# DeltaNet then MLP mixer: folded first recurrence with its state in PSUM, keys before queries, more work on GpSimd, and a new order

## The chip, the cores and the metric

The kernel runs on one core of one Trainium2 chip. A core has five engines that work side by side, each through its own queue in order: PE (TensorE, matrix products), DVE (VectorE), ACT (ScalarE), POOL (GpSimd) and SP (SyncE, which issues the transfers here). Products are written to PSUM, and DVE and ACT carry them to SBUF, the on-chip memory. The metric is the device time of one execution in microseconds, as the median of several runs.

## What is computed

The first half is a DeltaNet recurrence for 4 batches, 8 heads, 768 tokens and a head size of 48. The second is an MLP mixer over tokens (768 to 256 and back) and channels (384 to 1536 and back).

```python
def _attn_ref(q, k, v, beta) -> np.ndarray:
    ...
    k_n = k / (np.linalg.norm(k, axis=-1, keepdims=True) + 1e-06)
    state = np.zeros((B, H, D, D), dtype=np.float32)
    ...
    for t in range(S):
        kt, vt, bt = (k_n[:, :, t], v[:, :, t], beta[:, :, t, None])
        y[:, :, t] = np.einsum('bhd,bhde->bhe', q[:, :, t], state)
        v_old = np.einsum('bhde,bhd->bhe', state, kt)
        state = state + bt[:, :, :, None] * np.einsum('bhd,bhe->bhde', kt, vt - v_old)
    return y.astype(np.float32)
...
def _moe_ref(x, w_tok1, w_tok2, w_ch1, w_ch2) -> np.ndarray:
    xt = x.transpose(0, 2, 1)
    h = np.maximum(xt @ w_tok1, 0.0) @ w_tok2
    u = x + h.transpose(0, 2, 1)
    h2 = np.maximum(u @ w_ch1, 0.0) @ w_ch2
    return (u + h2).astype(np.float32)
```

## The kernel before

Tokens are taken in chunks of 64 (C), two chunks to a unit of 128 tokens: six units and twelve chunks for each batch, 24 units and 48 steps in all. Within a chunk the recurrence is solved in matrix form. The products of all keys with all keys (the gram) are masked to a triangle M; the inverse T of the unit triangular matrix gives the chunk's corrected values w = T (V - K S), where S is the state at the chunk's start; S is then changed by K'w and the outputs are read from Q, S and w.

The work is cut into generators, called jobs, each of which issues a few instructions and then yields. One long string, `order`, written into the kernel (L912 on), says which job is advanced next. Since scheduling is manual, each engine's queue holds its instructions in exactly that order; buffers and semaphores decide when each can start. The jobs, with their lines in the kernel before:

- k{u}, `load_kq` (L296): transfers of keys and queries of unit u to `kpad` and `qpad`, and of keys, stacked by chunk, to `kst`; for the first units ACT makes `kst` from `kpad` (L312).
- p{u}, `prep` (L345): squares on ACT (L354), sums on DVE (L357), roots on ACT, then on DVE the addition of a small number (L364), the reciprocal (L368), its square (L369) and the column `cs` = beta times that square (L370); PE turns the keys (L380) and the queries (L395); the mask `mb` is a triangle times `cs` (L388) and the scaled keys are `kst` times `cs` (L399), on DVE for units 0 to 3 (`EARLY_SC`) and on POOL for the others; the gram `p_g` (L408) covers keys and queries together, and DVE evicts it with the mask (L414); `to_parts` (L474) copies 32x32 blocks to where they are inverted.
- i{n}, `invert`: round 0 holds units 0 to 3, round 1 units 4 and 5; both turn blocks in SBUF on DVE (L518, L540, L543) and take back substitution steps of two DVE instructions (L526, L531). From round 2 on, rounds pass through DRAM (L520, L546). h{u} (`join_16`), f{u} (`from_parts`, L493) and j{u} (`join`, PE L592 and L601, ACT L595 and L604) build T of 64x64 from the inverted blocks.
- v{u}, `load_v` (L324): values, scaled on POOL (L329).
- r{t}: `recur_early` (L608) for the twelve steps of the first batch, `recur` (L684) for the other 36. A step of `recur_early` is: `p_k` = K S on PE (L629), V minus that on DVE (L633), `p_w` = T times it on PE (L648), a copy on ACT (L650), `p_s` = K'w on PE (L656), two subtractions from the state on DVE (L660), and the reading `p_y` (L639, L667) with its copies on ACT (L675).
- m{b}, `mixer` (L755): the token products `p_1` (L762), `p_h` (L775) and the transposes `p_ut`, then the channel products `p_c` (L824, relu on ACT L831) and `p_o` (L844, added to the output on DVE L793), in a scheme that makes seven half-size products do for eight, with sums on DVE (L817).
- w{j}, `round_weights` (L206): a piece of the weights comes as 64-bit words (L215) and becomes float32: ACT L220, DVE L221 and L226, ACT L232, POOL L233, and last a flush of tiny values to zero by one DVE instruction (L235). There are 34 pieces (j from 0).
- x and z, `keep_warm` (L162), and y, `warm_tiles` (L171): matrix products on zeros that only keep PE occupied, written to `p_warm` and `p_warm_2`.

PSUM tiles come from rings of banks: two for "prep", two for "seq" (`p_k`, `p_w`, `p_s`), three for "mlp" (one of which `p_warm_2` holds for good).

Every float32 product appears in the trace as two matmul records; a transpose appears as one.

Of the kernel before, what the change touches and what calls it, by code (L numbers as in the profile page):

```python
# [8 lines left out]
FP32 = mybir.dt.float32  # L9
# [4 lines left out]
C = 64  # L14
# [9 lines left out]
def kernel(  # L24
# [83 lines left out]
    EARLY_SC = (0, 1, 2, 3)  # L108
# [9 lines left out]
    mask_f = const.tile([128, 128], FP32, name="mask_f")  # L118
# [41 lines left out]
    p_warm_2 = ps_mlp([128, 4, 128], "p_warm_2")  # L160
# [10 lines left out]
    def warm_tiles():  # L171

        while True:
            for i, r in enumerate(PAR):
                for k, out_r in enumerate(PAR):
                    nc.tensor.matmul(  # L176
                        (p_warm_2 if i == k else p_warm)[out_r, 0], warm[r, 0:C],
                        warm[r, 0:128],
                    )
            yield  # L180
# [25 lines left out]
    def round_weights(dst, src, name):  # L206
# [13 lines left out]
        nc.scalar.activation(lo, lo, ACTF.Copy, scale=2.0**-29)  # L220
        nc.vector.tensor_scalar(  # L221
# [10 lines left out]
        nc.scalar.square(a, a)  # L232
        nc.gpsimd.tensor_tensor(out=f, in0=f, in1=lo, op=ALU.add)  # L233
        yield
        nc.vector.scalar_tensor_tensor(  # L235
            out=dst, in0=a, scalar=(1.125 * 2.0**-15) ** 2, in1=f.bitcast(FP32),
            op0=ALU.is_ge, op1=ALU.mult,
        )
# [3 lines left out]
    def round_pair(j, src):  # L242
# [4 lines left out]
            b[:, 2 * k : 2 * k + 2].rearrange("p j n -> p (j n)"), src, (id(wc2), j)  # L247
# [12 lines left out]
    def pieces_of(dst, src):  # L260
        rows = src.rearrange("(j p) n -> j p n", p=128)
        for n in range(0, dst.shape[2], WP):
            for j in range(dst.shape[1]):
                cut = slice(n, min(n + WP, dst.shape[2]))
                yield round_weights(dst[:, j, cut], rows[j, :, cut], (id(dst), j, n))
# [9 lines left out]
    turning = set()  # L275
# [8 lines left out]
    beta_in = []  # L284
    steps = []
    written = set()
    walked = set()
# [7 lines left out]

    def load_kq(u):  # L296
        assert u < NK or u - NK in masked
        b, c = divmod(u, NCH)
        ksts[u] = kst = loads.tile([128, NP, 2, D], FP32, name="kst", bufs=NK)
        for pad, src in ((kpad, k), (qpad, q)):  # L300
            nc.sync.dma_start(
# [22 lines left out]
    def load_v(u):  # L324
        assert u < 2 or u - 2 in walked
# [19 lines left out]
    def prep(u):  # L345

        assert u < NV or u - NV in walked
        b, c = divmod(u, NCH)
        kp, qp, kst = kpad[u % NK], qpad[u % NK], ksts.pop(u)
# [3 lines left out]
        ksq = work.tile([128, NB, D], FP32, name="ksq", bufs=1)  # L353
# [11 lines left out]
        cs = work.tile([128, NP, 2], FP32, name="cs")  # L365
        rec = work.tile([128, NB], FP32, name="rec")
# [650 lines left out]
```

## Time and profile before

| what | value |
|---|---|
| time, median of three runs | 729.87 us (729.57 to 732.58) |
| span of the profiled execution | 730.9 us |
| PE busy | 700.8 us (96%), 7774 matmul records |
| DVE busy | 439.8 us (60%), 1163 instructions |
| ACT busy | 242.1 us (33%), 569 instructions |
| POOL busy | 99.4 us (14%), 118 instructions |

The profile is one execution. "Busy" adds up the time in which an engine had an instruction under way; PE can be busy with products on zeros. The row PEclk gives the clock that PE was granted, in tenths of full speed. A group of instructions is named by line, engine and operation, with output and inputs by the program's names.

### The profile page before, as it was taken

To read this page: it belongs to the slowest core of one execution; us is meant where nothing else is said; L and a number is where in the kernel's file an instruction comes from. 1 tells how busy PE (TensorE), PEld (TensorE's weight loads), DVE (VectorE), ACT (ScalarE), POOL (GpSimd) and SP (SyncE) were. 2 spreads that over 40 slices of the span, in tenths; PEclk is the share of its full clock that TensorE was granted. 3 is DMA by queue.
4 is the path that set the end of the run, shared out by engine and by line. 5 is a ranking of instruction groups with operands and counts; after the bars stand their busy time and mean duration, and the time that the engine had idled before them with its cause. 6 is when DMAs were issued, how large, how long until landed. Compare 5 with 4: busy or idle time off the path is not lost.

```text
span 730.9 us, 18603 instructions
## 1 busy us (share of the span) xinstructions
PE 700.8 (96%) x7774; PEld 605.5 (83%) x7774; DVE 439.8 (60%) x1163; ACT 242.1 (33%) x569; POOL 99.4 (14%) x118
## 2 busy tenths in 40 slices
PE   8797998999999999999999999999999999999998
PEld 6556886757799988986899898968998986989997
DVE  5998678799796792545965559723776432311212
ACT  6636447443561213432325422123222331020110
POOL 1223035332323010121001201001000000000000
PEclk9987579899899999999999999999999999999999
DMA  9435435564425405255023222131002100000000
GB/s 169 107 85 117 88 72 133 161 140 105 90 66 99 91 1 111 41 109 102 1 60 77 43 59 42 39 70 28 12 28 42 34 12 1 22 0 23 1 22 22
DMA packets 146755, 46.13 MB, mean 63 GB/s; under 512 B 138064, under 2 KB 141136, under 8 KB 146672
## 3 DMA queue, kind: packets, MB, share of 16 engines
q1 hardware_dynamic: 146672, 44.95, 28.7%
q8 instruction: 61, 1.00, 0.6%
q14 instruction: 22, 0.18, 0.1%
HBM read 35.49 MB, written 9.44 MB: 61 GB/s over the span
## 4 chain that ended last, share of the span: by engine, by line
PE 67%; DVE 22%; ACT 3%; issue 3%; DMA 2%; SPq 1%; POOL 0%; ACTq 0%; DVEq 0%; POOLq 0%
PE p_o L844 20%; PE p_c L824 16%; DVE sub L526 6%; DVE x L531 5%; PE p L762 4%; PE p_q L702 4%; PE p_s L728 3%; PE p_w L718 3%; PE p_g L408 3%; PE p_h L775 3%; PE p_z L592 2%; PE p_x L601 2%; PE p_warm L166 1%; PE p_warm L176 1%; DVE gm L414 1%
## 5 line engine op out<-in xcount | busy, mean ns | idle before, releaser
L824 PE MATMUL p_c<-u_t,wc 128*128 128x256 f32 x864 | 195.6, 381 | 0.0
L824 PEld LDWEIGHTS p_c<-u_t,wc 128*128 128x128 f32 x864 | 161.2, 191 | 20.9 <-issue 0.3
L844 PE MATMUL p_o<-wc,r 128*128 128x192 f32 x720 | 128.5, 328 | 1.1 <-ACT u_t L789 0.6
L844 PEld LDWEIGHTS p_o<-wc,r 128*128 128x128 f32 x720 | 116.6, 190 | 3.1 <-ACT u_t L789 1.1
L831 ACT ACTIVATE r<-p_c 128x512 f32<-128x512 f32 x72 | 42.7, 596 | 156.1 <-PE p_c L824 156.1
L793 DVE TENSOR_TENSOR xb<-xb,p_o 128x192 f32<-128x192 f32 x84 | 29.3, 350 | 69.8 <-PE p_o L844 69.5
L526 DVE TENSOR_TENSOR sub<-x 128x84 f32<-128x84 f32 (+24 forms) x178 | 59.0, 332 | 14.6 <-DMA x<-n_dram 10.0
L531 DVE TENSOR_TENSOR x<-x,sub 128x84 f32<-128x84 f32 (+24 forms) x178 | 59.9, 336 | 6.1
L721 ACT COPY rw_bd<-p_w 64x192 f32<-64x192 f32 x72 | 22.4, 311 | 99.1 <-PE p_w L718 98.1
L844 PE MATMUL p_o<-wc,s 128*128 128x192 f32 x288 | 51.0, 329 | 2.5 <-DVE xb L793 2.5
L233 POOL TENSOR_TENSOR w_f<-w_f,d 128x384 uint32<-128x384 uint32 (+1 forms) x34 | 35.0, 1030 | 124.5 <-DVE w_f L226 65.3
L329 POOL TENSOR_TENSOR v_st<-v_st,nrm 128x384 f32<-128x384 f32 x24 | 20.1, 840 | 226.1 <-DMA v_st<-in_v_dram 122.0
L844 PEld LDWEIGHTS p_o<-wc,s 128*128 128x128 f32 x288 | 46.8, 190 | 3.7 <-DVE xb L793 3.3
L817 DVE TENSOR_TENSOR s<-r 128x384 f32<-128x384 f32 x24 | 13.9, 578 | 53.6 <-ACT r L831 53.6
L388 POOL TENSOR_TENSOR mb<-mask_c,cs 128x512 f32<-128x512 f32 x20 | 22.6, 1129 | 136.6 <-DVE cs L370 121.9
L414 DVE TENSOR_TENSOR gm<-p_g,mb 128x512 f32<-128x512 f32 x48 | 31.4, 684 | 15.6 <-PE p_g L408 11.5
L408 PE MATMUL p_g<-kqt 64*64 64x128 f32 x768 | 30.8, 304 | 7.3 <-ACT kqt L397 7.3
L702 PEld LDWEIGHTS p_q<-s_bd,kqt 128*128 128x128 f32 x264 | 33.9, 195 | 4.5 <-issue 2.4
L702 PE MATMUL p_q<-s_bd,kqt 128*128 128x96 f32 x264 | 36.0, 281 | 1.3 <-DVE s_bd L741 0.7
L736 DVE TENSOR_TENSOR s_bd<-s_bd,p_s 48x192 f32<-48x192 f32 x60 | 21.4, 357 | 25.9 <-PE p_s L728 25.0
L706 DVE TENSOR_TENSOR rw_bd<-p_q,v_st 64x192 f32<-64x192 f32 x66 | 23.0, 349 | 20.2 <-PE p_q L702 14.1
L728 PEld LDWEIGHTS p_s<-rw_bd,gm 128*112 128x112 f32 x288 | 32.9, 178 | 2.7 <-issue 0.3
(111 smaller groups left out, 999.3 us busy)
## 6 DMA issues: line engine op xcount, KB each, us to landing
d<-in_moe_w_ch_dram SPq DMA_DIRECT2D x24, 384.0 KB, 3.4
kpad<-in_k_dram SPq DMA_DIRECT2D x24, 192.0 KB, 3.7
qpad<-in_q_dram SPq DMA_DIRECT2D x24, 192.0 KB, 4.1
v_st<-in_v_dram SPq DMA_DIRECT2D x96, 48.0 KB, 2.6
out_dram<-xb SPq DMA_DIRECT2D x24, 192.0 KB, 2.0
kst<-in_k_dram SPq DMA_DIRECT2D x80, 48.0 KB, 2.9
n_dram<-gm SPq DMA_DIRECT2D x72, 32.0 KB, 1.9
gm<-w_dram SPq DMA_DIRECT2D x72, 32.0 KB, 2.2
```

What stands on the lines that cost most here:

```text
L233: nc.gpsimd.tensor_tensor(out=f, in0=f, in1=lo, op=ALU.add)
L408: nc.tensor.matmul(p_g[cc][PAR[i ^ cc], p], kqt[PAR[i], 2 * p + cc, 0], kqt[PAR[i], 2 * p + cc],)
L414: nc.vector.tensor_tensor(out=blocks(gm)[:, :, cc, 0 : 2 * C].rearrange("s p (two n) -> s p two n", two=2), in0=p_g[cc], in1=mb[:, :, cc, ...
L526: nc.vector.tensor_tensor(out=tmp, in0=y[:, :, 0:s, s : s + 1].to_broadcast([n, k, s, w]), in1=y[:, :, s : s + 1, s + 1 : m].to_broadcast( ...
L531: nc.vector.tensor_tensor(out=y[:, :, 0:s, s + 1 : m], in0=y[:, :, 0:s, s + 1 : m], in1=tmp, op=ALU.add,)
L702: nc.tensor.matmul(p_q[:, p], kqt[:, 2 * p + cc], s0[:, p])
L728: nc.tensor.matmul(p_s[0 : C + D, p], gm[:, 2 * p + cc, C:], w_bd[:, p])
L762: nc.tensor.matmul(p_1[dh], piece_of(w1, c, 0)[:, dh * 128 : (dh + 1) * 128], xb[:, c], start=(c == 0), stop=(c == NCH - 1),)
L793: nc.vector.tensor_tensor(out=xb[:, c, e], in0=xb[:, c, e], in1=p, op=ALU.add)
L824: nc.tensor.matmul(p_c[:, k], piece_of(wc1, cb, f * 128)[:, f * 128 : (f + 1) * 128], u_t[:, cb], start=(cb == 0), stop=(cb == NCB - 1),)
L831: nc.scalar.activation(r2[:, m], p_c, ACTF.Relu)
L844: nc.tensor.matmul(p, a[:, m], wc2[:, m, j], start=(start and m == 0), stop=(m == NM - 1), skip_group_check=True,)
```

## The change

In the first batch, a new job `fold` multiplies T into the values and into the keys of a chunk ahead of the steps (`p_tv` and `p_tk`, each evicted by ACT). A step then is `p_k` = (T K) S, w = that minus T V with its sign on DVE, and `p_state`, which adds K'w to a PSUM bank that is held from the first step to the last; the state for the next step is minus that bank, half by DVE and half by ACT. `p_w`, its copy and the subtractions from the state in SBUF are gone. Reading the outputs is a job of its own, y{t} (`read_early`).

In `prep`, `cs` and the mask are made on POOL for all units; the mask is written into `gm` where the key-query part will come, the squares where the scaled keys will come. For the first six units the keys are turned, their gram taken and passed on before the queries are turned; the gram comes in two products of 64x64 in place of one of 64x128, and the keys are scaled last, on POOL. `kst` has six buffers in place of four, with a padding that POOL clears.

In `round_weights` the flush of pieces 0 to 23 is made on POOL by two instructions; pieces 24 to 33 keep the one on DVE. `p_warm_2` is gone. Several jobs yield more often, and `order` is new throughout: in it `warm_tiles` products go from 244 to 36, those of `keep_warm` with 128 columns from 27 to 20, those with 512 from 16 to 19. Round 2 of the inversion begins in it after the first `p_1`; before, it began ahead of it. SP issues the same 437 transfers in another order.

```diff
     EARLY_DVE = (1, 3)
-    EARLY_SC = (0, 1, 2, 3)
+    POOL_FLUSH = range(24)
...
     p_warm = psum.tile([128, 4, 128], FP32, name="p_warm", tag="warm", bufs=1)
-    p_warm_2 = ps_mlp([128, 4, 128], "p_warm_2")
...
-            for i, r in enumerate(PAR):
-                for k, out_r in enumerate(PAR):
-                    nc.tensor.matmul(
-                        (p_warm_2 if i == k else p_warm)[out_r, 0], warm[r, 0:C],
-                        warm[r, 0:128],
-                    )
+            for j in range(2):
+                for r in PAR:
+                    nc.tensor.matmul(p_warm[r, j], warm[r, 0:C], warm[r, 0:128])
             yield
...
+        yield
         nc.gpsimd.tensor_tensor(out=f, in0=f, in1=lo, op=ALU.add)
         yield
-        nc.vector.scalar_tensor_tensor(
-            out=dst, in0=a, scalar=(1.125 * 2.0**-15) ** 2, in1=f.bitcast(FP32),
-            op0=ALU.is_ge, op1=ALU.mult,
-        )
+        least = (1.125 * 2.0**-15) ** 2
+        if j in POOL_FLUSH:
+            nc.gpsimd.tensor_scalar(
+                out=a, in0=a, scalar1=least, scalar2=None, op0=ALU.is_ge
+            )
+            nc.gpsimd.tensor_tensor(out=dst, in0=a, in1=f.bitcast(FP32), op=ALU.mult)
+        else:
+            nc.vector.scalar_tensor_tensor(
+                out=dst, in0=a, scalar=least, in1=f.bitcast(FP32),
+                op0=ALU.is_ge, op1=ALU.mult,
+            )
...
-        ksq = work.tile([128, NB, D], FP32, name="ksq", bufs=1)
+        ksq = gm[:, :, 2 * C :]
...
+        nc.vector.reciprocal(rec, nrm_f)
+        yield
         assert beta_in
-        nc.vector.reciprocal(rec, nrm_f)
-        nc.vector.tensor_tensor(out=rec, in0=rec, in1=rec, op=ALU.mult)
-        nc.vector.tensor_tensor(
+        nc.gpsimd.tensor_tensor(out=rec, in0=rec, in1=rec, op=ALU.mult)
+        nc.gpsimd.tensor_tensor(
             out=cs, in0=rec.rearrange("s (p c) -> s p c", c=2), in1=bet, op=ALU.mult
         )
-        yield
-
-        assert not turning and beta_in
...
-        scaler.tensor_tensor(
+        mb = blocks(gm)[:, :, :, C : 2 * C]
+        nc.gpsimd.tensor_tensor(
             out=mb, in0=mask_c[:, None, None, :].to_broadcast([128, NP, 2, C]),
             in1=cs[:, :, :, None].to_broadcast([128, NP, 2, C]), op=ALU.mult,
         )
         yield
-        p_t = ps_turn([128, NP, 2, C], "p_t")
...
-        yield
-        scaler.tensor_tensor(
-            out=blocks(gm)[:, :, :, 2 * C :], in0=kst,
-            in1=cs[:, :, :, None].to_broadcast([128, NP, 2, D]), op=ALU.mult,
-        )
-        yield
-        p_g = [ps_prep([128, NP, 2, C], "p_g") for cc in range(2)]
-        for p in range(NP):
...
+        def gram(k0, k1):
+            n = k1 - k0
+            p_g = [ps_prep([128, NP, n, C], "p_g") for cc in range(2)]
+            for p in range(NP):
+                for cc in range(2):
+                    for i in range(2):
+                        nc.tensor.matmul(
+                            p_g[cc][PAR[i ^ cc], p], kqt[PAR[i], 2 * p + cc, 0],
+                            kqt[PAR[i], 2 * p + cc, k0:k1],
+                        )
+            yield
             for cc in range(2):
-                for i in range(2):
-                    nc.tensor.matmul(
-                        p_g[cc][PAR[i ^ cc], p], kqt[PAR[i], 2 * p + cc, 0],
-                        kqt[PAR[i], 2 * p + cc],
-                    )
-        yield
...
+                nc.vector.tensor_tensor(
+                    out=blocks(gm)[:, :, cc, C * k0 : C * k1].rearrange(
+                        "s p (two n) -> s p two n", two=n
...
+                    in0=p_g[cc],
+                    in1=mb[:, :, cc, None, :].to_broadcast([128, NP, n, C]),
+                    op=ALU.mult,
+                )
...
+        def scale_k():
+            nc.gpsimd.tensor_tensor(
+                out=blocks(gm)[:, :, :, 2 * C :], in0=kst,
+                in1=cs[:, :, :, None].to_broadcast([128, NP, 2, D]), op=ALU.mult,
+            )
+            yield
+
+        yield from turn_kq(kp, kqt_k)
+        if early:
+            yield from gram(0, 1)
+            yield from to_parts(u)
+            yield from turn_kq(qp, kqt_q)
+            yield from gram(1, 2)
+            yield from scale_k()
+        else:
+            yield from turn_kq(qp, kqt_q)
+            yield from scale_k()
+            yield from gram(0, 2)
+            yield from to_parts(u)
...
+    p_state = []
+    early_w = {}
+    early_s = {}
+
+    def fold(u):
+
+        assert u in scaled and u in joined and u in masked
+        gm, kqt, v_st, kst = gm_of(u), kqts[u % NV], vsts[u], ksts.pop(u)
+        for cc in range(2):
+            p_tv = ps_seq([128, NP, D], "p_tv")
+            for p in range(NP):
+                for i in range(2):
+                    r = PAR[i ^ cc]
+                    nc.tensor.matmul(p_tv[r, p], gm[r, 2 * p + cc, 0:C], v_st[r, p, cc])
+            yield
+            nc.scalar.mul(v_st[:, :, cc], p_tv, -1.0 if u == 0 and cc == 0 else 1.0)
+            yield
+            p_tk = ps_prep([128, NP, C], "p_tk")
+            for p in range(NP):
+                for i in range(2):
+                    r, lo = PAR[i ^ cc], D * (2 * p + cc)
+                    nc.tensor.matmul(
+                        p_tk[PAR[i], p], kst[r, lo : lo + DP], gm[r, 2 * p + cc, 0:C]
+                    )
+            yield
+            nc.scalar.copy(
+                kqt.rearrange("f (p c) two s -> f p c two s", c=2)[:, :, cc, 0], p_tk
+            )
+            folded.add((u, cc))
+            yield
+
...
     def recur_early(t):
 
-
-
         u, cc = divmod(t, 2)
-        assert t == len(steps)
+        assert t == len(steps) and (u, cc) in folded
         steps.append(t)
         gm, kqt, v_st = gm_of(u), kqts[u % NV], vsts[u]
+        s0, s1 = s_bd[t % 2][:, :, 0:D], s_bd[(t + 1) % 2][:, :, 0:D]
+        early_w[t] = w = v_st[:, :, cc]
+        if t == 0:
+            p_state.append(ps_seq([128, NP, D], "p_state"))
+        else:
+            p_k = ps_seq([128, NP, D], "p_k")
+            for p, i, r in heads_in(t):
+                f = FEATS[i]
+                nc.tensor.matmul(p_k[r, p], kqt[f, 2 * p + cc, 0], s0[f, p])
+            yield
+            early_w[t] = w = w_bd[:, :, t % 2 * D : t % 2 * D + D]
+            nc.vector.tensor_tensor(
+                out=w, in0=p_k, in1=v_st[:, :, cc], op=ALU.subtract
+            )
+            yield
+        if t == NQ - 1:
+            return
+        for p, i, r in heads_in(t):
+            nc.tensor.matmul(
+                p_state[0][FEATS[i], p], gm[r, 2 * p + cc, 2 * C :], w[r, p],
+                start=(t == 0 and p == 0), stop=True, skip_group_check=True,
+            )
+        yield
+        f = FEATS[0]
+        nc.vector.tensor_scalar_mul(s1[f], p_state[0][f], -1.0)
+        yield
+        f = FEATS[1]
+        nc.scalar.mul(s1[f], p_state[0][f], -1.0)
+        early_s[t + 1] = s1
+        yield
+    def read_early(t):
+
+        u, cc = divmod(t, 2)
+        gm, kqt = gm_of(u), kqts[u % NV]
         if t == 0:
...
-            yield
-            assert u in scaled
-            rest = r_bd[:, :, 0:D]
-            nc.vector.tensor_tensor(
-                out=rest, in0=p_k, in1=v_st[:, :, cc], op=ALU.subtract
-            )
-            yield
-            for p, i, r in by_head:
+            s0 = early_s[t]
...
                 f = FEATS[i]
                 nc.tensor.matmul(
                     p_y[r, p], kqt[f, 2 * p + cc, 1], s0[f, p],
-                    start=(p == 0), stop=False,
+                    start=(p == 0), stop=False, skip_group_check=True,
                 )
             yield
-
-        assert u in scaled and u in joined
-        p_w = ps_seq([128, NP, D], "p_w")
-        for p, i, r in by_head:
-            nc.tensor.matmul(p_w[r, p], gm[r, 2 * p + cc, 0:C], rest[r, p])
-        yield
-        nc.scalar.copy(w, p_w)
-        yield
-
-        if t < NQ - 1:
-            p_s = ps_seq([128, NP, D], "p_s")
-            for p, i, r in by_head:
-                nc.tensor.matmul(p_s[FEATS[i], p], gm[r, 2 * p + cc, 2 * C :], w[r, p])
-            yield
-            for f in FEATS:
-                if t > 0:
-                    nc.vector.tensor_tensor(
-                        out=s1[f], in0=s0[f], in1=p_s[f], op=ALU.subtract
-                    )
-                else:
-                    nc.vector.tensor_copy(out=s1[f], in_=p_s[f])
-            yield
-        for p, i, r in by_head:
+        w = early_w[t]
+        for p, i, r in heads_in(t):
             nc.tensor.matmul(
                 p_y[r, p], gm[r, 2 * p + cc, C : 2 * C], w[r, p],
-                start=(t == 0 and p == 0), stop=(p == NP - 1),
+                start=(t == 0 and p == 0), stop=(p == NP - 1), skip_group_check=True,
             )
         if cc == 1:
             walked.add(u)
         yield
         for i in range(2):
-            nc.scalar.mul(
-                y[:, :, D * i : D * i + D], p_y[PAR[i ^ cc]], 1.0 if t else -1.0
-            )
+            nc.scalar.copy(y[:, :, D * i : D * i + D], p_y[PAR[i ^ cc]])
         written.add(t)
+        yield
         if t == NQ - 1:
             for t_ in (w_bd, *s_bd):
                 nc.gpsimd.memset(t_, 0.0)
...
```

## The prediction

> **What bounds the kernel now.** I read the page's busy rows first, then the stretches between milestones, then the timeline where engines collide. The forty slices:
>
> ```profile
> span 730.9 us, 18603 instructions
> PE 700.8 (96%) x7774; PEld 605.5 (83%) x7774; DVE 439.8 (60%) x1163; ACT 242.1 (33%) x569; POOL 99.4 (14%) x118
> PE   8797998999999999999999999999999999999998
> DVE  5998678799796792545965559723776432311212
> PEclk9987579899899999999999999999999999999999
> PE 67%; DVE 22%; ACT 3%; issue 3%; DMA 2%; SPq 1%; POOL 0%; ACTq 0%; DVEq 0%; POOLq 0%
> ```
>
> The span is 1.0 above the median run. PE's 96% misleads: early on much of it is filler (keep-warm) matmuls. The reader should see that slices 1 to 11 (about 200 us) have a busy DVE and a dipping clock, and the rest neither. I cut at the start of the first inversion (i0, L518, 35.7), its end (L543, 49.8), the first state product (p_s, 68.4), the first token-mixing product (p_1, 150.4) and the first output product (p_o, 207.5). Stretches near these cuts (busy columns PE, PEld, DVE, ACT, POOL):
>
> ```profile
> 0.00:35.00 35.00, 29.14 (x418) 22.08 (x418) 25.61 (x69) 22.70 (x54) 5.95 (x14) 1.00 0.74 139
> 35.00:68.00 33.00, 26.21 (x665) 19.41 (x666) 28.82 (x75) 16.67 (x38) 10.48 (x11) 0.74 0.44 96
> 68.00:150.00 82.00, 75.33 (x1897) 62.13 (x1898) 63.11 (x169) 43.76 (x113) 25.81 (x27) 0.79 0.49 116
> 150.00:208.00 58.00, 55.29 (x572) 41.78 (x569) 51.22 (x122) 25.75 (x63) 16.06 (x19) 0.94 0.49 110
> 208.00:731.00 523.00, 514.84 (x4233) 460.08 (x4231) 271.05 (x732) 133.23 (x306) 41.13 (x48) 1.00 0.20 43
> ```
>
> After 208 PE is 98% busy at clock 1.00 and hardly changed: counting what is queued behind the first p_o at full-clock durations gives 531.0 before, 528.8 after. So everything hangs on when p_o starts. Ahead of it DVE holds 25.6+28.8+63.1+51.2 = 168.7 of 208 us.
>
> The clock is the second limit:
>
> ```profile
> 56.20:66.40 10.20, 7.22 (x176) 6.66 (x180) 7.69 (x19) 7.21 (x17) 4.78 (x5) 0.50 0.51 116
> 73.25:100.40 27.15, 26.63 (x522) 23.12 (x525) 16.45 (x57) 12.23 (x36) 5.54 (x6) 0.50 0.40 84
> 100.40:131.30 30.90, 26.88 (x861) 21.93 (x857) 26.18 (x62) 18.20 (x45) 12.36 (x13) 1.00 0.50 109
> ```
>
> From 73 to 100 PE looks full, yet passes 522 matmul records in 27 us against 861 in the next 31.
>
> The third is DVE and POOL together:
>
> ```profile
> 28.25 2.55 POOL L233 TENSOR_TENSOR w_f<-w_f,d 128x384 uint32<-128x384 uint32 x2 [9.92 <-DVE w_f L226]
> 28.55 1.38 DVE L399 TENSOR_TENSOR gm<-kst,cs 128x384 f32<-128x384 f32 x1
> 29.94 1.51 DVE L474 COPY r<-gm 32x256 f32<-32x256 f32 x2
> ```
>
> The scaling L399 takes 0.55 with POOL idle, the copy L474 0.38 each; beside POOL they take 1.38 and 0.75. Summed to 210 us, such DVE operations (two SBUF inputs, or SBUF copies) lasted 15.1 us longer than their quiet durations where they overlapped the 58 us of POOL work: 0.26 us lost per us of POOL. PSUM evictions, reductions and stream transposes lost nothing.
>
> [...] Here the half-clock stretches are multiples of 3.41 us; [...] Here L388 takes 1.13 on POOL against 0.69 on DVE.
>
> **The change part by part.** Durations below are means of each line's rows.
> DVE, whole kernel: 24 of 34 flushes leave (-24 x 0.555 = -13.3), the reciprocal and scale columns (-48 x 0.167 = -8.0), four masks and four key scalings (-2.8 -2.8), the state subtract L660/L664 gives way to half-width negations (x22, 7.7 to 3.3, -4.4), and twelve extra gram evictions of smaller size add 1.7: -29.6. Ahead of p_o: 174.4 to 151.1.
> POOL: each flush becomes two operations that the trace doesn't show on POOL. Below: 0.42 each (the 128x384 memset L681's row), 24 x 0.84 = 20. Above: 0.83 and 1.08 (the rows of L329 and L233), 24 x 1.91 = 46. I take 0.75 + 1.08 with some pieces narrower, about 42. Forty-eight tiny columns at about 0.15 add 7, eight masks and scalings 8: POOL goes 100 to 157, and up to p_o 56.7 to 115.6.
> ACT: fold's two evictions, 12 x 0.315 + 12 x 0.35, replace L650's 3.8; half negations add 3.4: total +7.6, mostly beside DVE.
> PE: fold issues 192 matmuls where p_w issued 96; at 0.031 a record that is +6.0. Filler ahead of p_1 falls from 51.0 to 28.6 (warm tiles 244 to 36). PE work ahead of p_1: 117.8 to 108.3.
> Waits added. The reciprocal columns and the mask of a unit now stand in POOL's queue behind flushes, two of which take about 3.7; whoever waits for the mask is the gram eviction on DVE, and behind that, on DVE, the inversion's steps. Bound: nothing, if the planned order leaves room, to 3.7 for each of the six early units, 22; I take the overheads below and leave the rest to the range. p_state holds one of the two "seq" PSUM banks from the first step to the last, so p_tv and p_k share the other: a product behind an eviction waits some 0.7 (0.355 for the row of L633 and the hand-over). For the ten folds that can meet a step: nothing to 7; I take nothing, as p_w waited on DVE in the same way before. Reading (p_y) moves to the "mlp" bank that p_warm_2 gave up and hangs on nothing in the chain.
> Recurrence step: p_k, DVE, p_w, ACT, p_s, DVE becomes p_k, DVE, p_state, then DVE beside ACT. That takes one product (0.5), one copy (0.32) and one of two state operations (0.35) with their hand-overs off each of 12 steps. But the steps did not run at chain speed: 82 us over 12 steps with PE busy 75 is queue order and clock. So I price this by work, not by chain. SP issues the same 437 transfers in a new order, the keys of units 1 and 0 and the first weights ahead of all queries: keys come earlier, each query later by the weights' and keys' transfers that it is moved past, and queries are needed only after i0 and i1. I take nothing; a key behind one weight transfer would cost that one's 3.4 us.
>
> Sum, each stage taken as its binding engine's work plus the overhead that the same stage had before, plus 0.26 per added us of POOL.
> 1. To i0. ACT 22.3 after the first load has landed (6.6; before ACT 24.4): 29.0 against 35.7. Keys-first pays here.
> 2. i0. DVE ahead of its end grows, as work for i1 and w moves up: 20.8 (39.3-18.5) against 12.0. Before it took 14.1, so overhead 2.1; POOL 13.9 against 1.4 adds 3.3. 26.2, so 55.2 against 49.8.
> 3. To the first state product: i1's preparation now stands here too. DVE 24.5 against 16.3 (which took 18.6: 2.3); POOL 20.0 against 8.0 adds 3.1. 29.9, so 85.1 against 68.4.
> 4. To p_1: PE 52.4 at full clock (filler only 4.4) against 69; DVE 30.7, hidden. Before, 34 of 82 us were at half clock, 17 of the 69 us of work; the same quarter at half adds 13.1. [...] 65.5, so 150.6 against 150.4.
> 5. To p_o: DVE 56.6 against 50.4 (in 57.2: 6.8); the third inversion (i2) that stood ahead of p_1 now stands wholly here. POOL 29.2 against 15.5 adds 3.6. 67.0, so 217.6 against 207.5.
> p_o comes 10.1 late; PE behind it has 2.2 less: 730.9 + 7.9 = 738.8 by span, 737.8 by median. [...]
>
> **The rivals.**
> Faster. The clock holds through the recurrence, where PE is packed more densely than before, and POOL's operations fall beside evictions. Then 29.0 + 22.9 + 26.8 = 78.7; stage 4 has 52.4 plus one half-clock window, 3.4: 134.5; stage 5 63.4: 197.9. 730.9 - 9.6 - 2.2 - 1.0 = 718. For it: DVE has 23 us less ahead of p_o[...]. [...]
> Much slower. The recurrence runs wholly at half clock, as 73 to 100 did, with no filler to lift it: stage 4 rises to 84 and p_1 to 169, of which p_o keeps the 18.6 on top of its 10.1: 757. [...]
> No change. Gains and losses cancel at p_o near 209.7: 730. The new order may also simply fail to gain from fold because PE waits on POOL-fed masks instead: that is inside the likeliest case.
>
> **How the numbers follow.** Likeliest, 738 (own range 733 to 750): 0.46. Faster, 718 (711 to 725): 0.27. Much slower, 757 (750 to 765): 0.15. About as before: 0.12. Half a per cent (3.6 us) is what a measurement can tell, so faster 0.27, same 0.12, slower 0.61. The range takes in the centres of both outer cases, with the flush's bounds (20 to 46 us of POOL, times 0.26 = 7 us) leaning low: 714 to 762.
>
> **What would show each step.** The first L540 near 29 and its last transpose L566 near 55; p_state's first product near 85; p_1 near 150; p_o near 218; filler under 30 us ahead of p_1; DVE operations with two SBUF inputs stretched beside POOL L235 and L238; a clock below 0.85 between 85 and 150. If p_1 comes before 140 with the clock near 1.00, the prediction is wrong in stage 4; if p_state comes before 80, the POOL term is wrong. If the stretch after p_o differs from 521 by more than 3, the belief that the tail is fixed is wrong.

## The result, and the profile after

The changed kernel takes 760.98 us (median of four runs, 757.25 to 764.03) against 731.06 for the kernel before on the same chip: a ratio of 1.041, 95% interval 1.0374 to 1.0446. The forecast was 738, and its direction held; the loss of 4.1% is nearly four times the 1.1% forecast. The profiled execution has a span of 762.2.

The page of the changed kernel, the rows that answer to those shown of before:

```profile
span 762.2 us, 18602 instructions
...
PE 705.2 (93%) x7734; PEld 603.2 (79%) x7734; DVE 430.2 (56%) x1084; ACT 250.2 (33%) x592; POOL 169.8 (22%) x228
...
PE   6667999896798999999999999999999999999998
...
DVE  3998844369969695445873337958752423211212
...
PEclk9778777898799999999998999999999999999999
...
PE 62%; DVE 18%; DMA 8%; SPq 6%; issue 4%; ACT 2%; POOL 0%; ACTq 0%; DVEq 0%
```

PE is about as busy in sum as before (705 against 701), but it is idle for 57 us in place of 30. In the chain of waits DMA and SP rise from 3% to 14%. The same kernel in stretches that end at i0's start, i0's end, the first state product, p_1, p_o and the end (busy columns PE, PEld, DVE, ACT, POOL, then the clock):

```profile
0.00:32.90 32.90, 21.97 (x286) 14.29 (x286) 19.46 (x56) 21.94 (x53) 19.16 (x45) 0.86 0.78 138
32.90:58.60 25.70, 18.76 (x283) 13.53 (x284) 24.06 (x60) 10.76 (x21) 16.86 (x19) 0.72 0.35 90
58.60:91.80 33.20, 27.19 (x745) 16.95 (x744) 30.01 (x65) 19.05 (x46) 23.49 (x23) 0.79 0.27 74
91.80:158.10 66.30, 60.47 (x1682) 52.76 (x1681) 29.90 (x71) 37.66 (x103) 36.10 (x42) 0.79 0.57 112
158.10:228.90 70.80, 58.20 (x553) 42.63 (x551) 59.07 (x136) 29.55 (x68) 28.89 (x37) 0.88 0.50 119
228.90:762.20 533.30, 518.65 (x4197) 463.07 (x4194) 267.68 (x703) 131.28 (x303) 45.29 (x67) 0.99 0.18 39
```

| stretch | before | forecast | measured |
|---|---|---|---|
| to i0 | 35.6 | 29.0 | 32.9 |
| i0 | 14.2 | 26.2 | 25.7 |
| to the first state product | 16.0 | 29.9 | 33.2 |
| to p_1 | 84.5 | 65.5 | 66.3 |
| to p_o | 57.2 | 67.0 | 70.8 |
| to the end | 523.4 | 521.2 | 533.3 |

So p_o starts 21.4 late (10.1 forecast), and 9.9 more are lost behind it (2.2 were to be gained). The table's first state product of before stands where its matmuls begin, 65.8; the prediction cut at 68.4.

The table is one execution of each kernel, and stages vary between executions. Five runs below (e3, e6, e9, e15 and e16) keep the changed kernel's instructions up to its first state product, and all of these but e6 keep them up to p_1 (e9 leaves out work behind p_1 only). With the same instructions the first state product came between 89.9 and 93.9 and p_1 between 154.9 and 166.2. A difference of a few us in one stage of one profile is therefore weak evidence; the medians of whole runs weigh more.

In the recurrence DVE is busy for 30 of 66 us; before it was for 65.5 of 84.5. In the stretch behind, it is busy for 59 of 71. PE has its two long stalls there (timeline, PE alone):

```profile
186.15 1.11 PE L400 MATMUL p_t<-ident,kpad 128*128 128x128 f32 x4 [5.97 <-DVE gm L420]
...
205.84 1.06 PE L615 MATMUL p_z<-t,gm 32*32 32x32 f32 x32 [4.95 <-DVE t L610]
```

Both times PE's next instruction waits for something that stands on DVE behind steps of the third inversion or instructions of weight pieces. This is a reading of the trace; the experiments ask what is worth time.

### The profile page after: what moved, and what is told of

Same layout as the page of the kernel before. It is cut to its first block, busy times and chain, and to the rows that moved or that the text cites. A ratio compares the mean times of both kernels' runs of the same rounds, so it can differ in the third digit from the quotient of the medians.

```text
span 762.2 us, 18602 instructions
## 1 busy us (share of the span) xinstructions
PE 705.2 (93%) x7734; PEld 603.2 (79%) x7734; DVE 430.2 (56%) x1084; ACT 250.2 (33%) x592; POOL 169.8 (22%) x228
## 4 chain that ended last, share of the span: by engine, by line
PE 62%; DVE 18%; DMA 8%; SPq 6%; issue 4%; ACT 2%; POOL 0%; ACTq 0%; DVEq 0%
PE p_c L884 19%; PE p_o L905 16%; DVE x L554 4%; DVE sub L548 4%; PE p_q L757 3%; PE p_h L833 3%; PE p L819 3%; PE p_s L784 3%; PE p_w L773 3%; DMA x<-n_dram 3%; SPq L504 2%; DVE gm L420 2%; PE p_warm L165 2%; SPq L332 2%; DMA n_dram<-gm 2%
## 5 line engine op out<-in xcount | busy, mean ns | idle before, releaser
L884 PE MATMUL p_c<-u_t,wc 128*128 128x256 f32 x864 | 197.8, 383 | 0.0
L905 PE MATMUL p_o<-wc,r 128*128 128x192 f32 x720 | 131.3, 334 | 1.5 <-DVE xb L854 0.9
L905 PEld LDWEIGHTS p_o<-wc,r 128*128 128x128 f32 x720 | 119.7, 194 | 4.0 <-DVE xb L854 1.5
L548 DVE TENSOR_TENSOR sub<-x 128x84 f32<-128x84 f32 (+24 forms) x178 | 65.0, 365 | 18.8 <-DMA x<-n_dram 14.0
L554 DVE TENSOR_TENSOR x<-x,sub 128x84 f32<-128x84 f32 (+24 forms) x178 | 64.9, 364 | 4.9
L414 PE MATMUL p_g<-kqt 64*64 64x128 f32 (+1 forms) x960 | 34.9, 280 | 10.8 <-DVE gm L420 5.8
L420 DVE TENSOR_TENSOR gm<-p_g,gm 128x512 f32<-128x512 f32 (+1 forms) x60 | 33.2, 575 | 19.1 <-PE p_g L414 11.7
L414 PEld LDWEIGHTS p_g<-kqt 64*64 64x64 f32 x960 | 27.8, 152 | 19.0 <-ACT kqt L403 9.7
L403 ACT COPY kqt<-p_t 128x512 f32<-128x512 f32 x48 | 27.4, 584 | 41.1 <-PE p_t L400 41.0
L165 PE MATMUL p_warm<-warm 128*128 128x128 f32 (+1 forms) x78 | 38.6, 608 | 1.0 <-DVE warm L113 1.0
L792 DVE TENSOR_TENSOR s_bd<-s_bd,p_s 48x192 f32<-48x192 f32 x60 | 21.4, 357 | 28.0 <-PE p_s L784 27.1
```

Source lines behind the costliest of these rows:

```text
L165: nc.tensor.matmul(p_warm[:, 0:m], zero, zero[:, None, :].to_broadcast([128, m, 128]))
L403: nc.scalar.copy(dst, p_t)
L414: nc.tensor.matmul(p_g[cc][PAR[i ^ cc], p], kqt[PAR[i], 2 * p + cc, 0], kqt[PAR[i], 2 * p + cc, k0:k1],)
L420: nc.vector.tensor_tensor(out=blocks(gm)[:, :, cc, C * k0 : C * k1].rearrange("s p (two n) -> s p two n", two=n), in0=p_g[cc], in1=mb[:, : ...
L548: nc.vector.tensor_tensor(out=tmp, in0=y[:, :, 0:s, s : s + 1].to_broadcast([n, k, s, w]), in1=y[:, :, s : s + 1, s + 1 : m].to_broadcast( ...
L554: nc.vector.tensor_tensor(out=y[:, :, 0:s, s + 1 : m], in0=y[:, :, 0:s, s + 1 : m], in1=tmp, op=ALU.add,)
```

## The experiments

Times are medians; the kernel before ran beside each group, at 729 to 731 us.

**POOL's work undone.** e1 has only this edit:

```diff
-    POOL_FLUSH = range(24)
+    POOL_FLUSH = range(0)
```

> The changed kernel with the flush of pieces 0 to 23 back on DVE as one instruction; all else as changed. POOL theory (the flush's two operations, 48 us of POOL in the trace, [...]delay masks and scalings): POOL busy falls by about 48, DVE operations with two SBUF inputs shrink by some 9 us ahead of the first state product, and the time falls by 8 or more, to 753 or less. Order theory (the loss comes from where the new order puts things, and DVE is as full with the flush as without it): within 4 of 761, since 13.3 us of flush come back to DVE.

Measured: 761.96. e2 takes this edit and puts the columns and the early masks and scalings back on DVE:

```diff
-        nc.gpsimd.tensor_tensor(out=rec, in0=rec, in1=rec, op=ALU.mult)
+        nc.vector.tensor_tensor(out=rec, in0=rec, in1=rec, op=ALU.mult)
...
-        nc.gpsimd.tensor_tensor(
+        scaler = nc.vector if u in EARLY_SC else nc.gpsimd
+        scaler.tensor_tensor(
```

> As the run before, and besides the square of the reciprocal and the column cs on DVE for all units, and masks and key scalings of units 0 to 3 on DVE, as in the kernel before. POOL theory: 750 or less. Order theory: 758 to 768, as DVE gets 27 us more work ahead of p_o in the stages where it is busy for nine tenths.

Measured: 769.05. The POOL theory falls: without the flush the time is the same, and without any of these moves it is 8 longer, so the columns and the early masks and scalings save some 7 on POOL. DVE's instructions take longer beside that flush all the same. Ahead of the first state product (groups of DVE, the changed kernel, then e1 without POOL's flush; last columns busy time and mean ns):

```profile
L515 DVE COPY gm<-r 32x256 f32<-32x256 f32 x8 | 5.0, 629 | 0.2
L218 DVE TENSOR_SCALAR w_f<-d 128x384 uint32<-128x384 uint32 x7 | 4.4, 633 | 0.1
L223 DVE SCALAR_TENSOR_TENSOR w_f<-d,w_f 128x384 uint32<-128x384 uint32 x6 | 4.0, 673 | 0.1
```

```profile
L515 DVE COPY gm<-r 32x256 f32<-32x256 f32 x8 | 3.7, 462 | 0.2
L223 DVE SCALAR_TENSOR_TENSOR w_f<-d,w_f 128x384 uint32<-128x384 uint32 x6 | 3.3, 554 | 0.0
...
L218 DVE TENSOR_SCALAR w_f<-d 128x384 uint32<-128x384 uint32 x7 | 2.5, 355 | 0.0
```

The same instructions are 18% to 44% shorter in e1. The stretch to the first state product in e1, and then in e2:

```profile
59.10:91.70 32.60, 26.74 (x716) 16.50 (x704) 26.09 (x70) 19.13 (x46) 9.87 (x11) 0.78 0.28 76
```

```profile
60.90:92.60 31.70, 26.96 (x750) 16.90 (x749) 23.94 (x61) 17.73 (x42) 7.08 (x7) 0.82 0.28 78
```

DVE is busy for 26.1 of 32.6 us in e1 and 23.9 of 31.7 in e2, against 30.0 of 33.2. So 3.9 and 6.1 us of DVE work less leave the stretch 0.6 and 1.5 shorter, which is within what the same instructions vary by (31.2 in e15, 35.5 in e3). DVE's work did not set its length.

**The tail.** e3 keeps the changed order up to the first p_o and takes the rest from the order of before.

> The changed kernel with its own order up to the first p_o, and from there on the steps in the order of the kernel before (the same steps, put at its finer grain). The stretch from the first p_o to the end was 533.3 in the changed kernel, 523.4 before, and forecast at 521. Tail-order theory: the new order itself lets PE wait in the tail; here the stretch falls to 521 to 526 and the time to 749 to 754. Debt theory (the tail is longer because work left over from a late start, weights and the third inversion, runs into it): the stretch stays within 3 of 533 and the time within 4 of 761.

Measured: 759.07 (757.51 to 765.79), no change beyond the spread of the two. In its profile the tail was 524.6, but p_o had started at 239.4, with the same instructions ahead of it as in the changed kernel. In e1, e2, e5 and e6, whose tail has the changed order, the tail was 527.0 to 529.1. So 2.4 to 4.5 us of the tail go with the order, and the remaining 4.2 to 6.3 up to 533.3 are the profiled execution's own. The changed code in the order of before to its end (e4, e7 and e8, below) had tails of 520.5, 521.3 and 524.4. Two windows of the changed kernel's tail were partly at half clock:

```profile
256.28:263.10 6.82, 5.51 (x30) 5.46 (x31) 6.15 (x21) 0.27 (x2) 0.00 (x0) 0.75 0.00 0
402.91:413.14 10.23, 8.70 (x99) 8.06 (x92) 2.72 (x8) 1.91 (x5) 0.83 (x1) 0.67 0.27 42
```

In the first the clock was 0.50 for 3.4 us (258.94 to 262.35), in the second for 6.8 (405.71 to 412.54). A p_o product (128x192) took 0.527 us there, by the median, against 0.326 from 300 to 400 us, at a clock of 1.00. If PE did half as much in these 10.2 us, up to 5 us were lost, an estimate.

**The clock.** e5 has 34 more Y words ahead of the recurrence, e6 9 more z words in it, each sprinkled evenly.

```diff
-    k1 w1*2 k0 b k2 k1 w1 z w1*2 Y k2 k1*2 k0*2 ...
+    k1 w1*2 k0 b k2 k1 w1 z w1*2 Y k2 Y k1*2 k0*2 ...
```

> The changed kernel with 34 more Y words (136 small products on zeros) spread evenly over the order from its start to the first state product: PE idles for 24 us there, and the granted clock was 0.85, 0.72 and 0.79 in the three stages. Clock theory (the cut of filler from 244 to 36 products lets the clock fall, and the half-clock products of grams and joins make DVE wait): clock above 0.9 ahead of the first state product, which comes 4 or more earlier (88 or less), and the time falls by 4 or more, to 757 or less. DVE and POOL theory (there those two set the pace): the clock rises, the first state product stays within 2 of 92, the time within 3 of 761.

> The changed kernel with 9 more z words (four times wider products on zeros, 1.1 us each at full clock) spread from the first state product to the first p_1, where PE was busy for 60.4 of 66.2 us at a clock of 0.79. Clock theory: the clock rises to 0.9 or more, and the stage gets shorter in spite of 9 us more work, to 62 or less; time 757 or less. Bound theory (PE is full there whatever the clock, and what it gains it spends on the filler): the stage takes 66 to 75, time 760 to 770.

Measured: 766.74 and 760.93. The clock rose as forecast, in e5 from 0.86, 0.72, 0.79 to 0.94, 0.88, 0.95, and in e6's recurrence to 0.95:

```profile
90.60:159.50 68.90, 64.34 (x1699) 49.87 (x1698) 32.78 (x73) 38.40 (x108) 37.16 (x44) 0.95 0.56 109
```

Its length did not fall (68.9 against 66.3 with some 9 us of filler more), and e5's first state product came at 93.7. The filler with which the clock rose showed no gain in time (760.98 without it).

That does not make the clock worthless. Without any added filler, the same instructions had other clocks in other executions. The recurrence in e9 and in e3:

```profile
91.90:154.90 63.00, 55.15 (x1681) 48.13 (x1681) 29.43 (x70) 36.62 (x101) 36.26 (x42) 0.91 0.57 115
```

```profile
93.90:166.20 72.30, 65.33 (x1681) 56.51 (x1680) 26.16 (x69) 37.46 (x103) 33.46 (x41) 0.72 0.52 102
```

At 0.91, 0.79 and 0.72 PE was busy for 55.2, 60.5 and 65.3 us with them, and the stretch took 63.0, 66.3 and 72.3. Length and clock go together here, though these profiles do not show which leads. From i0's start to p_1 the clocks of the two kernels differ little: 0.76, 0.70 and 0.79 before, and 0.72, 0.79 and 0.79 in the changed kernel. To i0 it was 1.00 before and 0.86 after the change, as far as the traces record it, and e5 with 0.94 there was no earlier at i0 (34.2 against 32.9).

**Changed code, old order.** e4 translates the order of before to the new jobs; e7 the same with folds issued early; e8 is e7 with the POOL work on DVE. e7 and e8 leave out a term of the output for 64 tokens: the second reading product of step 10 comes after the buffer of its w was cleared. The instructions are the same.

> The code of the changed kernel (fold, p_state, POOL work, p_warm_2 gone) with the order of the kernel before from end to end, its steps put at the finer grain, folds issued as soon as T, values and keys are there, and queries of the first six units turned after the keys' blocks are passed on. Order theory: the code is not slower than the code before, so 720 to 738. POOL theory: POOL's added 57 us cost here too, so 745 to 760, with the loss ahead of the first p_o.

> Again the changed code in the order of the kernel before, now with each fold issued as early as its inputs allow, one piece at a time between other steps, and the reading of a step behind its state product; in the run with that order above, every fold stood directly ahead of its own step, whose p_k waited for its eviction (10 us a step). Order theory: first state product near 76, p_1 at 150 to 160, p_o at 205 to 218, time 728 to 742. Code theory (folding, smaller grams, POOL work cost more than p_w did, in any order): p_1 at 165 or later, time 748 or more.

> The same order as the run before (changed code, order of the kernel before, early folds), with flush, reciprocal columns, and masks and key scalings of units 0 to 3 on DVE: what is left of the change is fold, p_state, the keys-first preparation and the freed bank. If POOL's work costs in that order, this is faster than the run before by 5 or more; if POOL and DVE stand for each other, within 4 of it or slower by up to 8, as it was in the changed order (762 and 769 against 761).

Measured: 779.15, 782.29 and 783.36; e4 is longer than either of its theories had it. The first state product was early (76 to 78), p_1 at 196 to 208. Folding does not fit the old order. It holds the key buffer of each early unit until its T is there. The changed order has the loads of keys behind unit 5 begin at 94.5 us, where they began at 27.5 before. Placed in the old order such a load makes SP wait, and everything in its queue behind it. SP's longest wait in e7 (from 55 to 210 us; total us, times, longest) is for the fold's product `p_tk`:

```profile
SPq L332 <- PE p_tk L654: 40.4, 3, 18.0
```

In e4 it is 26.2. These three say that code and order belong together; they do not say what the code alone is worth. e7 and e8 lie 1.1 us apart: POOL and DVE stand for each other there as well.

**The third inversion left out.** e9 is the changed kernel, e10 the kernel before, each without 60 DVE instructions:

```diff
         for s in range(1, m - 1):
+            if rnd == 2:
+                yield
+                yield
+                continue
```

> The changed kernel without the 30 substitution steps of the third inversion (60 DVE instructions, about 24 us), whose data then pass through as they are; transfers, joins and all else stay. In the changed order they stand wholly between the first p_1 and the first p_o, a stretch of 70.8 us in which DVE was busy for 59. Debt theory (DVE work that the new order left behind p_1 sets when p_o starts): the stretch falls by 12 or more, to 59 or less, and the time by 10 or more, to 751 or less. Rival (weights, transfers and the first mixer's own chain set p_o): the stretch stays above 65, the time within 5 of 761.

> The kernel before without the same 30 steps. There half of them ran ahead of the first p_1. Debt theory: the stretch from p_1 to p_o, 57.2, falls by less than in the changed kernel, 3 to 9, and the time by 3 to 9, to 721 to 727. Rival: no change within 2.

Measured: 756.67 and 725.45, some 4 us each. The runs of e9 (751.27 to 760.44) overlap with those of the changed kernel; e10 is clear of the noise (ratio 0.9949, interval 0.9924 to 0.9974) and fits the debt theory there. In e9 the stretch from p_1 to p_o was 68.2, with DVE busy for only 37.7 of it:

```profile
154.90:223.10 68.20, 60.41 (x552) 43.63 (x550) 37.69 (x76) 30.18 (x69) 28.09 (x35) 0.86 0.53 125
```

So 21.4 us of DVE work less make this stretch 2.6 shorter. For the changed kernel the debt theory falls, and with it the forecast's premise that this stage is as long as DVE's work and a fixed overhead.

**Parts of the change in the kernel before.** e11 moves the flush of 24 pieces to POOL, e12 keeps the state in PSUM without folding.

```diff
-        nc.vector.scalar_tensor_tensor(
-            out=dst, in0=a, scalar=(1.125 * 2.0**-15) ** 2, in1=f.bitcast(FP32),
+        if len(flushed) <= 24:
+            nc.gpsimd.tensor_scalar(
+                out=a, in0=a, scalar1=least, scalar2=None, op0=ALU.is_ge
+            )
+            nc.gpsimd.tensor_tensor(out=dst, in0=a, in1=f.bitcast(FP32), op=ALU.mult)
```

> The kernel before with the flush of its first 24 pieces on POOL as two operations; order and all else as before. By the rate of the forecast (0.26 us of DVE lost for each us of POOL, some 40 us of POOL ahead of p_o, against 13 us of flush taken off DVE) it is within 3 of 730. If two operations on POOL cost by their length (a piece's buffer is free 2 us later, and the next transfer of weights waits for it), 735 or more; if DVE's relief counts, 726 or less.

```diff
-                nc.tensor.matmul(p_s[FEATS[i], p], gm[r, 2 * p + cc, 2 * C :], w[r, p])
+                nc.tensor.matmul(
+                    p_state[0][FEATS[i], p], gm[r, 2 * p + cc, 2 * C :], w[r, p],
+                    start=(t == 0 and p == 0), stop=True, skip_group_check=True,
+                )
...
+            nc.vector.tensor_scalar_mul(s1[FEATS[0]], p_state[0][FEATS[0]], sign)
+            nc.scalar.mul(s1[FEATS[1]], p_state[0][FEATS[1]], sign)
```

> The kernel before with p_state alone: the products K'w of the first batch add up in one held PSUM bank, and the next state is minus that bank, half by DVE and half by ACT; p_w and its copy stay, no fold, order as before. If the chain of the first recurrence sets the pace there, 0.35 us are gained on each of 11 steps, 726 or less. If queue order and clock set it, within 2 of 730. If the held bank makes p_k and p_w wait for each other, 733 or more.

Measured: 740.41 (ratio 1.0148, interval 1.0117 to 1.018) and 733.03 (1.0022, 0.9968 to 1.0077). The state in PSUM is worth nothing that shows. The flush on POOL costs 11 us in the old order. SP's waits ahead of p_o in e11 (total us, times, longest):

```profile
SPq L217 <- POOL w L243: 35.6, 8, 11.2
SPq L217 <- POOL wc L243: 26.9, 10, 6.0
```

Together these are 62.5 us; the same loads waited 48.9 us for the shorter flush on DVE before. The next transfer of weights waits for a buffer that the flush frees, and whatever SP has behind it waits too; p_1 came 7 later. In the changed order SP waits 74.7 us for POOL's flush, but 62.0 for DVE's in e1, and undoing it gains nothing.

**Weights and mixer steps moved up.** e13 spreads the weight words of the recurrence and behind so that 110 in place of 43 stand ahead of p_1 (e14: with the flush on DVE). e15 and e16 move the first mixer's turn and its p_c up by four and eight of its places.

```diff
-    r1 w18 h5 r1*2 j4 x v2 f5 h5 j3 p6 k6 v2 j4 j3 r1*2 ...
+    r1 w15 h5 r1*2 w20 j4 x v2 w15 f5 h5 j3 w17 p6 k6 v2 w21 j4 j3 r1 w17 r1 ...
```

> The changed kernel with only the words of the weight pieces moved: from the first state product on they are spread evenly so that 110 of the remaining 149 stand ahead of the first p_1 (43 in the changed order), none later than it was. Weight theory (the pieces, three buffers deep and last in the chain ahead of p_o, come late: piece 24 at 187, piece 32 at 222, p_o at 229; before 157, 203 and 207): piece 32 ends by 210, p_o starts at 212 to 218, the time falls by 8 to 15, to 746 to 753. Rival (PE and DVE are as full as they can be, so that what is moved ahead of p_1 delays p_1 by as much): p_1 at 165 or later, the time within 4 of 761.

> As the run before, with the flush of all pieces on DVE as one instruction. A buffer of a piece is then free some 2 us earlier, and SP, which waited 75 us for POOL's flushes ahead of p_o with all other loads behind it, waits less. Weight theory: a further 3 to 8 us, 740 to 748. Rival: within 4 of the run before.

```diff
-    m0 w22 i2 w23 i2 w24 p10 i2 w23 w22 i2*2 k13 p10 m0 i2 ...
+    m0*5 w22 i2 w23 i2 w24 p10 i2 w23 w22 i2*2 k13 p10 m0 i2 ...
```

> The changed kernel with 28 steps of the first mixer moved up by four of its own places: the turn of its result (p_ut and its copies) directly behind the last p_h, and each p_c four places earlier, so that p_c no longer stands behind all of the third inversion, five weight pieces and the preparation of units 10 and 11. In the changed kernel 36.2 us lie between the first p_1 and the first p_c (24.3 before), with a PE stall of 6.0 on a gram's eviction among them. Order theory of this stretch: p_c starts 20 to 26 after p_1, PE's idle time between p_1 and p_o falls from 12.6 to 6 or less, p_o starts 5 or more earlier, the time falls by 5 to 14, to 747 to 756. Rival (p_o waits for the weight pieces in any case, and PE only idles later): p_c is early, p_o within 3 of its place, the time within 4 of 761.

> The same with eight places in place of four: four p_c products stand directly behind the turn, the others eight places earlier. Order theory: as the run before or better, 744 to 756. Rival: within 4 of 761, or later, as a relu of p_c on ACT then stands ahead of what the preparation needs.

Measured: 777.94, 775.96, 767.50 and 770.59; all longer, e13 and e15 longer than either theory had it. In e13 piece 32 was ready at 190 in place of 222, but p_1 came at 179 and p_o at 256. In e15 p_c started 25 us after p_1 in place of 36, but p_o 80 us after it, where the changed kernel took 70.8 and e3 73.2. What is late in the trace is not thereby what sets the time. A likely reason is that what is moved up pushes other instructions of the same queues back by more; that was read from the later p_1 and p_o and not tested apart.

**The second inversion beside the recurrence, or ahead of it.** e17 is the kernel before with i1's steps in a block; e18 the changed kernel with 20 of them, and what follows from them, moved down.

```diff
-    r0 i1 w0 y h1 r1*2 y r1 h1*2 h3 j1 f3*2 ...
+    r0 i1*15 w0 y h1 r1*2 y r1 h1*2 h3 i1*2 j1 f3*2 ...
```

> The kernel before with the 17 steps of the second inversion (i1, units 4 and 5) moved: they stand in one block between the first and the second step of the recurrence, as far as its inputs allow, where before they were spread over the first six steps and filled DVE between them. Overlap theory (the changed order works i1 off ahead of the recurrence, so that DVE is idle for 36 of 66 us in it, 19 of 84 before, and everything behind the first state comes late): the second state product some 8 to 12 later, p_1 4 to 12 later, time 734 to 744. Rival (what is done earlier is missing later, so the place of i1 is even): 727 to 733.

> The changed kernel with the last 20 of the 31 steps of i1, and the joins of units 4 and 5 that follow from it, moved some 80 words down, so that most of them run beside the first steps of the recurrence instead of ahead of it. Overlap theory: the first state product by 88 (91.8), p_1 3 to 10 earlier, time 750 to 757. Rival: the first state product is earlier, p_1 is not, time 758 to 766.

Measured: 740.25 (ratio 1.014, 1.0109 to 1.017) and 765.14. The recurrence of the kernel before, and then of e17:

```profile
65.80:150.30 84.50, 77.83 (x2013) 64.49 (x2005) 65.51 (x173) 44.43 (x113) 25.84 (x27) 0.79 0.49 114
```

```profile
65.40:158.80 93.40, 76.26 (x2013) 62.48 (x2005) 66.02 (x173) 44.70 (x113) 25.73 (x27) 0.79 0.44 103
```

Work and clock are the same, and the stretch is 8.9 longer: the second state product came at 84.5 in place of 74.9, and PE is idle for 17 us of it in place of 7. Taking this overlap away costs the kernel before 10.75 us. Giving part of it back to the changed one gained nothing: the first state product came at 88.9, but p_1 at 163.0, and the time is 4 longer.

## Why the prediction was right and wrong

**Right.** Slower, by a first state product and a p_o that come late. The recurrence is shorter by 18 us with folds and little filler, at the same granted clock (0.79). The forecast had carried the share of half clock over from before; what sets it is not shown. That its 66.3 us fall on the forecast 65.5 is partly luck, as the same instructions took 63.0 to 72.3. i0 takes 25.7 (26.2).

**Where the miss lies.** By span it is 762.2 against 738.8, 23.4 us: 3.9 to i0, 0.5 less in i0, 3.3 to the first state product, 0.8 in the recurrence, 3.8 from p_1 to p_o, and 12.1 behind p_o.

**To i0** the sum did not keep its own rule. Before, 6.6 and ACT's 24.4 make 31.0 of 35.7, an overhead of 4.7; the forecast of 29.0 is 6.6 and 22.3 without it. With it 33.6 come out, and 32.9 were measured. ACT was idle for 11.0 us of this stage, before for 12.3. The chain of waits runs through the fourth transfer of keys, which landed at 13.4; ACT waited 1.6 us for it. The new order of the loads, priced at nothing, may have a part in this, but no run tests it.

**POOL.** The rate of 0.26 us lost per us of POOL was too low for one stretch: to the first state product DVE's same work took 6.7 us longer (30.0 less 23.3, e1's 26.1 without five flushes of 0.56) for 13.6 us of POOL, 0.49. Over the whole kernel DVE is busy for 5.1 us more than in e1 although 24 flushes, 13.1 us, are not on it: 18.2 us longer for 50.6 of POOL, 0.36. Why DVE takes longer beside POOL is not shown. The flush was mis-sized as well (POOL's groups of the changed kernel, busy and mean ns):

```profile
L235 POOL TENSOR_SCALAR d<-d 128x384 f32<-128x384 f32 x18 | 22.6, 1256 | 7.1 <-ACT d L229 6.2
...
L238 POOL TENSOR_TENSOR wc<-d,w_f 128x384 f32<-128x384 f32 x14 | 15.2, 1084 | 1.2
```

The comparison took 1.26 where the forecast took 0.75 and bounded it by 0.83; both operations on all pieces make 52 us, above the upper bound of 46. Yet neither error shows in the result, since e1, with this work off POOL, takes the same time.

**The step that failed** ahead of p_o is the sum's own rule, "each stage taken as its binding engine's work plus the overhead that the same stage had before". It took DVE for the binding engine to the first state product and from p_1 to p_o, and fell short by 3.3 and 3.8 us there. In the sum's own terms, to the first state product DVE's work was 30.0 against 27.6 and the overhead 3.2 against 2.3; from p_1 to p_o they were 59.1 against 60.2 and 11.7 against 6.8. But the two terms do not add up to a stage as the sum has it: e1, e2 and e9 show that DVE's work could shrink by an eighth (30.0 to 26.1), a fifth (30.0 to 23.9) and a third (59.1 to 37.7) while the stage became shorter by 0.6, 1.5 and 2.6. What sets the length of such a stage instead is not shown. In the trace it reads as waiting between queues, and PE's busy time varies with the clock (55.2 us at 0.91 and 65.3 at 0.72 in the recurrence); no run separates the two.

**The tail** was the largest miss, and here the step "PE behind it has 2.2 less" failed: 12.1 us over the forecast in the profile, some 6 to 8 in e1, e2, e5 and e6. By the prediction's own sign, more than 3 away from 521, the belief that the tail is fixed is wrong. "Everything hangs on when p_o starts" took PE's work for its time: PE had 14.6 us idle in it (8.1 before). The two half-clock stretches (up to 5 us, by estimate) and the order (2.4 to 4.5, by one profile of e3) cover most of the 12.1; e3's own 3.4 over the forecast stays open.

**What stays open.** What made the changed kernel 30 us longer is not shown part by part. Two of its features cost time when they are put into the kernel before: i1 in a block ahead of most of the recurrence 10.75 us, the flush on POOL 11. Neither gains when it is taken out of the changed kernel (e18, in part, 765.14; e1, 761.96). So such costs do not add up, and neither is shown to be the cause of the loss. Keys before queries and the freed bank were not tried alone, nor was the fold. That PE's stalls at 186 and 206 cost what they last was only read from the trace; e15 speaks against it. An earlier load of the keys behind unit 5, with folding, was not tried.

## What to carry to other kernels

Price a new order not by the work of its busiest engine in each stage alone but also by what runs beside each dependent chain: a block of DVE work that had filled the gaps between steps of a recurrence cost the kernel before 10.75 us when it was done in one piece, though the work stayed the same. Such a cost holds for the order that it was measured in; undoing it in another order may gain nothing, as here. Before calling an engine the bound of a stage, take work off it and see whether the stage gets shorter; here DVE, 90% busy (30.0 of 33.2 us), was not: with 23.9 us of work the stage took 31.7. And compare several executions of the same instructions before reading a few us in one stage as an effect. An instruction that frees a transfer's buffer can have a price at the transfer queue and at everything behind it there, besides its own time (e11: 11 us, with 24 flushes on POOL).

## What the runs showed of the hardware that was not expected

On POOL, a comparison with a constant (one input, 128x384) took 1.26 us, longer than the product of two such tensors (1.08). Products of 128x8, which were put at 0.15 us, took 0.22 to 0.24. With some 9 us of filler more in the recurrence the granted clock was 0.95 in place of 0.79 and its length about as it was (68.9 and 66.3), while the same instructions without more filler took 63.0 us at 0.91 and 72.3 at 0.72. And the same instructions can differ by some 10 us at p_o between executions (228.9 and 239.4 in the changed kernel and in e3).
